# Block means of v from a second copy of v, added up on GpSimd

## The chip, the cores and the metric

The kernel runs on one core of a Trainium2 chip. The metric is the device time of one execution in microseconds (us), the median of several runs. Engines are named as the profile names them: PE is TensorE's matmul, PEld its weight load, DVE is VectorE, ACT is ScalarE, POOL is GpSimd, SP is SyncE, which issues most DMAs. An engine works through its own queue in order.

## The reference

Attention with a local window and block summaries, then a mixture of experts with greedy routing. Cut to what matters here:

```python
q, k, v: (4 batches, 8 heads, 768 positions, 64), float32
k_sum = k.reshape(B, H, 24, 32, 64).max(axis=3)     # 24 blocks of 32 positions
v_sum = v.reshape(B, H, 24, 32, 64).mean(axis=3)    # the block means
scores_l = scale * q @ k.T, only where |i - j| < 16
scores_s = scale * q @ k_sum.T + log(32)
a = softmax(concat([scores_l, scores_s]))
attn = a @ concat([v, v_sum])
# then: x = attn, 3072 rows of 512; logits = x @ w_gate (8 experts);
# greedy assignment, 384 rows for each expert; out = relu(x @ w1[e]) @ w2[e]
```

The change touches only how v_sum is worked out.

## The kernel before

Attention works on units u of 64 positions, 12 for a batch, 48 in all, in pairs that make a tile t of 128 positions, 24 in all. A unit sees 24 block keys and a window of 94 keys, so 118 columns. For every tile PE does the scores (task "s", line 316, 32 matmul records with 4 head pairs, 2 units, 2 halves and two passes), a transpose of the exponentials for each unit ("t", line 135), the value matmuls ("pv", line 352, tile names o0 and o1), a transpose of the output ("xt", line 135) and the routing logits ("l", line 358). DVE masks the scores and takes their maximum ("m", line 324), and normalises the output ("n", lines 378 to 381); ACT does the exponentials ("e", line 331). The copy of a transposed unit ("c", lines 175 and 177, which are in a helper) goes to ACT or DVE. A value matmul of tile t waits for "n" of tile t-1, since one pair of PSUM banks serves all tiles.

The windows of v lie in VW, one buffer for even and one for odd batches: rows 0 to 23 hold the 24 block means, rows 24 to 119 a unit's 96 positions of v, loaded by one DMA for each unit ("w", line 304, 195 KB). A 65th column of ones in each head gives the softmax sum.

The block means of a batch, for each half of the heads g: "vm" (lines 267 to 273), 12 matmuls over the loaded windows that add up the 32 positions of each block (in PSUM at four times 32 rows, 24 records in the profile since float32 takes two passes); "vmc", a copy to SBUF; "vb" (line 283), one matmul that puts the rows in block order; "vbc", a copy to rows 0 to 23 of unit 0. After the second half "place" (line 292) copies these rows on POOL to the other 11 units. So vm needs all 12 windows of its batch. Both halves take turns in the one PSUM bank "x", which the output transposes use too.

For each batch POOL also copies key windows ("win", 128x1128, line 177) and block maxima ("ks", 128x288, line 177) for batches 1 to 3, and issues the store of every output tile ("xw", line 418) to DRAM. The maxima themselves are DVE's ("max", line 252). Loads for the next batch run while a batch is worked on: q by one DMA of 1536 KB (batch 0 in three of 512 KB), k by four of 399 KB.

The order of the instructions on every engine is written by a planner (line 142): it keeps a list of tasks with an engine, a cost, dependencies and a rank, and takes, engine by engine, what can start earliest, and among those within a slack the lowest rank. The numbers in TUNE are ranks' offsets, slacks and the planner's lead LA. After attention come the routing rounds and the experts (lines 441 to 774); the change doesn't touch them.

Of the kernel before, what the change touches and what calls it, by code (L numbers as in the profile page):

```python
# [23 lines left out]
NB = S // BLK  # L24
# [13 lines left out]
    y2m=0.021, y3=1.7, y4=1.5, y5=1.6, y7=1.1, lo=1.1, sp=1.6, qx=23.421, aw=9.0, as_=2.6,  # L38
    ap=1.6, qf=8.3981, xw=5.4012, fp=2.4, ql=21.2102, mm=0.174, my=0.228, wlo=1.6, xlo=1.1, LA=4.6, PT=7, 
    sm=4, spe=0, sdve=0.327, sact=0.018, spool=0, m=0.309, e=1.649, t=1.965, c=0.695,  # L40
    n=0.518, xt=3.377, xf=3.627, l=5.806, k=18.158, q=15.15, vm=5, mx=9.243, back=3.94, w=12, qa=-11.877, qb=1.082, cut=22,
    cs=0.19, ct=0.45, cp=0.54, cx=0.45, cl=0.42, wend=22.685, wstart=1.0, wfrac=0.538,
# [6 lines left out]
CO = 128 + 3 * C  # L49
CA = CO + 96 + NB  # L50
CW = CA + E + 224
# [5 lines left out]
def attention_moe(ctx, tc, qT, kT, v65, wg, w1r, w2r, cst, out, dbg=None, dbi=None):  # L57
# [123 lines left out]
    with ExitStack() as att:  # L181
# [3 lines left out]
        VW = [sb.tile([128, NQ, H, VD], F32, name=f"vw{i}") for i in range(2)]  # L185
        kd, kw, VP, VM, VB, KS, SM, PS, PE_, PP, PT, PO, XS, XP, XTS, PL = ({} for _ in range(16))
        cuts = [0, 8, 16, TUNE['cut'], 24]
# [47 lines left out]
        for b in range(B):  # L235
# [7 lines left out]
            for p in range(HP):  # L243
# [19 lines left out]
                def _(eng=None, b=b, p=p):  # L263
                    copy(eng or nc.gpsimd, kw[b, p][:, :, :NB], KS[b, p][:, None, :].to_broadcast([128, NQ, NB]))

            for g in range(2):
                @task(("vm", b, g), "pe", 1.6, [("w", u0 + i) for i in range(NQ)] + ["constants"]
                      + ([("vbc", b, 0)] if g else [("xf", u0 // 2 - 4)] if b else []), u0 - TUNE["vm"] + 0.1 * g)
                def _(b=b, g=g):
                    VP[b, g] = psum.tile([128, 512], F32, name="x")[:, :4 * VD]  # L270
                    for k in range(3):
                        for j in range(4):
                            nc.tensor.matmul(VP[b, g][32 * j:32 * j + 32], own[:C, k], VW[b % 2][:C, 4 * k + j, 4 * g:4 * g + 4].rearrange("k h d -> k (h d)"), start=k == 0, stop=k == 2)  # L273

                @task(("vmc", b, g), {"act": 0.42, "dve": 0.4}, None, [("vm", b, g)], u0 - TUNE["vm"])
                def _(eng, b=b, g=g):
                    VM[b, g] = sb.tile([128, 4 * VD], F32, name="vm", bufs=2)
                    copy(eng, VM[b, g], VP[b, g])

                @task(("vb", b, g), "pe", 0.45, [("vmc", b, g)], u0 - TUNE["vm"])  # L280
                def _(b=b, g=g):
                    VB[b, g] = psum.tile([128, 512], F32, name="x")[:NB, :4 * VD]
                    nc.tensor.matmul(VB[b, g], blocks, VM[b, g], start=True, stop=True)
# [497 lines left out]
def _layouts(q, k, v, moe_w_gate, moe_w1, moe_w2):  # L781
# [69 lines left out]
```

## Time and profile before

| | |
|---|---|
| time, median of 3 runs | 503.75 us (500.2 to 506.34) |
| time of the profiled execution | 499.47 us |
| its span, first to last instruction | 497.7 us |
| busy: PE, PEld | 458.6 us (92%), 388.6 us (78%) |
| busy: DVE, ACT, POOL | 330.8 us (66%), 218.1 us (44%), 125.6 us (25%) |
| granted TensorE clock, mean | 0.957 |
| attention part | to about 139 us |

The page gives busy time by engine and a strip of 40 slices; the trace can be asked for busy time in a given stretch, for the chain of work that ended last, for an engine's instructions in order of time, and for groups of equal instructions with the mean time of one. A piece in a timeline may merge several instructions; "x24" is their number. Brackets at its end tell how long the engine was idle before it, and what ended that.

### The profile page before, as it was taken

How to read it: one execution, taken by the hardware profiler on the slowest of the kernel's cores; microseconds unless marked ns; L12 is line 12 of the kernel's file. 1: busy time of each engine (PE TensorE's matmuls, PEld its weight loads, DVE VectorE, ACT ScalarE, POOL GpSimd, SP SyncE). 2: the span in 40 equal slices, each digit the busy share in tenths (PEclk: the TensorE clock that was granted, in tenths of full speed). 3: DMA queues.
4: the chain of work that ended last, by engine and by line, in shares of the span. 5: the costliest groups of instructions: out<-in, count | busy, mean ns of one | idle time of the engine just before them, and what ended most of it. 6: DMA issues, size and time to landing. Idle time of an engine off the chain costs nothing.

```text
span 497.7 us, 13114 instructions
## 1 busy us (share of the span) xinstructions
PE 458.6 (92%) x5161; PEld 388.6 (78%) x5161; DVE 330.8 (66%) x1295; ACT 218.1 (44%) x454; POOL 125.6 (25%) x193
## 2 busy tenths in 40 slices
PE   5989999999945799989999999999998999999993
PEld 5568786878835798679779868978986998988982
DVE  4587989978767678749949867696795462461510
ACT  5575765877701433324324413333341553453410
POOL 9392745416122000121023005003100501302011
PEclk9998999999965799989999999999998999999998
DMA  8999978111203704615607408443434553621001
GB/s 273 320 325 375 297 244 265 67 66 45 87 24 136 267 1 171 233 63 183 221 28 257 184 1 296 128 161 119 146 110 146 165 175 138 197 88 63 2 21 42
DMA packets 24156, 76.27 MB, mean 153 GB/s; under 512 B 3488, under 2 KB 3744, under 8 KB 23712
## 3 DMA queue, kind: packets, MB, share of 16 engines
q1 hardware_dynamic: 18336, 56.58, 34.5%
q0 software_dynamic: 5760, 18.88, 10.8%
q8 instruction: 40, 0.66, 0.5%
q14 instruction: 20, 0.16, 0.1%
HBM read 62.86 MB, written 12.58 MB: 152 GB/s over the span
## 4 chain that ended last, share of the span: by engine, by line
PE 70%; DVE 11%; issue 8%; DMA 7%; SPq 2%; POOL 1%; POOLq 0%; ACT 0%; DVEq 0%; ACTq 0%
PE h L754 23%; PE y L771 18%; PE r L453 5%; PE o L352 5%; DMA vw<-v 5%; PE t L135 5%; PE s L316 4%; PE l L358 2%; PE x L135 2%; PE xt L135 2%; DMA xg<-xd,idx 2%; DVE al L598 2%; PE x L273 1%; DVE g L107 1%; SPq L304 1%
## 5 line engine op out<-in xcount | busy, mean ns | idle before, releaser
L771 PE MATMUL y<-bl,hh 128*128 128x512 f32 x192 | 79.0, 412 | 0.0
L737 POOL DMA_INDIRECT out<-y,idx x24 | 23.7, 986 | 215.7 <-ACT y L735 214.0
L771 PE MATMUL y<-bh,hl 128*128 128x512 f32 x192 | 77.5, 403 | 0.0
L771 PE MATMUL y<-bh,hh 128*128 128x512 f32 x192 | 77.1, 402 | 0.0
L758 ACT ACTIVATE hh<-h 128x384 fp32r<-128x384 f32 x64 | 31.5, 492 | 89.4 <-PE h L754 82.7
L331 ACT ACTIVATE pe<-sm,mx 128x118 f32<-128x118 f32 x192 | 57.6, 383 | 7.1 <-DVE mx L324 7.0
L754 PE MATMUL h<-xh,ah 128*128 128x384 f32 x256 | 58.4, 346 | 0.0
L754 PE MATMUL h<-xl,ah 128*128 128x384 f32 x256 | 58.3, 342 | 0.0
L754 PE MATMUL h<-xh,al 128*128 128x384 f32 x256 | 57.7, 344 | 0.0
L761 DVE SCALAR_TENSOR_TENSOR hl<-h,hh 128x384 fp32r<-128x384 f32 x64 | 35.3, 552 | 32.5 <-ACT hh L758 32.5
L629 ACT ACTIVATE xh<-xt 128x384 fp32r<-128x384 f32 x28 | 13.7, 491 | 80.8 <-PE xt L135 80.8
L754 PEld LDWEIGHTS h<-xh,ah 128*128 128x128 f32 x256 | 46.3, 192 | 0.7
L324 DVE CUSTOM_DVE_ANT_0 sm<-s,cs 128x118 f32<-128x118 f32 x192 | 40.6, 276 | 8.6 <-PE s L316 7.3
L754 PEld LDWEIGHTS h<-xh,al 128*128 128x128 f32 x256 | 45.6, 191 | 0.0
L754 PEld LDWEIGHTS h<-xl,ah 128*128 128x128 f32 x256 | 45.2, 189 | 0.0
L609 POOL DMA_INDIRECT xg<-xd,idx x24 | 24.1, 1003 | 79.9 <-DVE L L518 34.8
L595 ACT ACTIVATE ah<-raw 128x1024 fp32r<-128x1024 f32 (+1 forms) x36 | 32.4, 958 | 26.1 <-DVE m L124 21.5
L771 PEld LDWEIGHTS y<-bh,hh 128*128 128x128 f32 x192 | 36.7, 191 | 7.0
L771 PEld LDWEIGHTS y<-bl,hh 128*128 128x128 f32 x192 | 36.8, 192 | 6.0
L771 PEld LDWEIGHTS y<-bh,hl 128*128 128x128 f32 x192 | 36.7, 191 | 5.8
L453 PEld LDWEIGHTS <-g 128*128 128x128 bf16 x1008 | 29.0, 97 | 15.6 <-DVE g L107 7.9
L598 DVE TENSOR_TENSOR al<-raw,ah 128x1024 fp32r<-128x1024 f32 (+1 forms) x36 | 38.4, 1099 | 0.8 <-ACT ah L595 0.8
(130 smaller groups left out, 784.4 us busy)
## 6 DMA issues: line engine op xcount, KB each, us to landing
raw<-w1r SPq DMA_DIRECT2D x32, 512.0 KB, 4.4
raw<-w2r SPq DMA_DIRECT2D x32, 512.0 KB, 4.2
vw<-v SPq DMA_DIRECT2D x48, 195.0 KB, 7.9
kd<-kT SPq DMA_DIRECT2D x16, 399.0 KB, 5.8
xd<-x POOLq DMA_DIRECT2D x24, 256.0 KB, 4.2
qt<-qT SPq DMA_DIRECT2D x3, 1536.0 KB, 12.8
qt<-qT SPq DMA_DIRECT2D x3, 512.0 KB, 5.8
xg<-xd,idx POOLq DMA_INDIRECT x24, 3.7
```

What stands on the lines that cost most here:

```text
L135: nc.tensor.transpose(o, i, idn)
L324: nc.vector.tensor_tensor_reduce(sm[:, p], PS[u][:, p], m, -0.125, 3e38, op0=OP.add, op1=OP.min, accum_out=mx[:, p:p + 1])
L331: nc.scalar.activation(PE_[u][:, p], SM[u][0][:, p], AF.Exp, bias=SM[u][1][:, p:p + 1], scale=-1.0)
L352: nc.tensor.matmul(po(t, s)[x * 64:x * 64 + 64, p], PT[u][:, p, x * 64:x * 64 + 64], VW[b % 2][:C, i - s + x, 2 * p + s], start=True, stop ...
L453: nc.tensor.matmul(pc, g[t // HT][:, t % HT * n:t % HT * n + 128], oh[:, t], start=t == 0, stop=t == NT - 1)
L595: nc.scalar.activation(hi[:, c], raw[:, c], AF.Copy)
L598: nc.vector.tensor_tensor(lo[:, c], raw[:, c], hi[:, c].bitcast(F32), op=OP.subtract)
L609: nc.gpsimd.indirect_dma_start(out=x, out_offset=None, in_=xd, in_offset=bass.IndirectOffsetOnAxis(ap=idx[:, c:c + 1], axis=0))
L754: nc.tensor.matmul(ph, a[:, d], b[:, d], start=n == 0, stop=n == 11)
L758: nc.scalar.activation(hh[:, f], ph, AF.Relu)
L761: nc.vector.scalar_tensor_tensor(hl[:, f], ph, 0.0, hh[:, f].bitcast(F32), op0=OP.max, op1=OP.subtract)
L771: nc.tensor.matmul(py[c], a[:, f, s], b, start=f == 0 and i == 0, stop=f == 7 and i == 2)
```

## The change

For batches 1 to 3, "vm" and "vmc" go. A new DMA ("vt", 96 rows of 16,640 bytes, 1.6 MB) brings the batch's v once more, each of 96 rows holding 8 neighbouring positions. POOL adds these 8 up in four instructions ("va"): 4 positions of 8 onto others in two adds of 1040 elements, then 2 onto 2, then 1 onto 1 (520 elements). One matmul for each half of the heads ("vb") then adds groups of four rows with the new constant `quarters` (24 columns, 1/32 each). So the windows are no longer needed for the means. Batch 0 keeps its way, but the second half of the heads uses the PSUM bank "l" rather than "x", and the SBUF copy uses the buffer "xr". Several TUNE numbers differ, among them LA, the ranks of the window loads (w) and key maxima (mx), and two slacks; they move tasks within the planner's order.

```diff
-    ... LA=4.6, PT=7, 
-    sm=4, spe=0, sdve=0.327, sact=0.018, spool=0, m=0.309, e=1.649, t=1.965, c=0.695,
-    n=0.518, xt=3.377, xf=3.627, l=5.806, k=18.158, q=15.15, vm=5, mx=9.243, back=3.94, w=12, ...
+    ... LA=6.154, PT=7, 
+    sm=4, spe=0.015, sdve=0.316, sact=0.358, spool=0, m=0.569, e=2.793, t=2.307, c=0.793,
+    n=0.518, xt=3.377, xf=3.104, l=5.806, k=18.109, q=16.26, vm=5, vt=12, va=8, mx=12.906, back=6.52, w=5.302, ...
...
-CA = CO + 96 + NB
+CA = CO + 96 + 2 * NB
...
-    blocks = cs[:, CO + 96:CA]
+    blocks, quarters = cs[:, CO + 96:CO + 96 + NB], cs[:96, CO + 96 + NB:CA]
...
+            if b:
+                @task(("vt", b), "sp", 0.48, [("vb", b - 1, 1)] if b > 1 else [], u0 - TUNE["vt"], 4.35)
+                def _(b=b):
+                    VT[b] = sb.tile([96, 8, H * VD], F32, name="vt")
+                    v = v65[b]
+                    nc.sync.dma_start(VT[b], bass.AP(tensor=v.tensor, offset=v.offset + HALO * H * VD, ap=[[8 * H * VD, 96], [H * VD, 8], [1, H * VD]]))
+
+                for k, (i, j, n) in enumerate(((0, 4, 2), (2, 6, 2), (0, 2, 2), (0, 1, 1))):
+                    @task(("va", b, k), "pool", 2.4 if n == 2 else 1.25, [("va", b, k - 1) if k else ("vt", b)], u0 - TUNE["va"])
+                    def _(b=b, i=i, j=j, n=n):
+                        nc.gpsimd.tensor_tensor(VT[b][:, i:i + n], VT[b][:, i:i + n], VT[b][:, j:j + n], op=OP.add)
+
             for g in range(2):
-                @task(("vm", b, g), "pe", 1.6, [("w", u0 + i) for i in range(NQ)] + ["constants"]
-                      + ([("vbc", b, 0)] if g else [("xf", u0 // 2 - 4)] if b else []), u0 - TUNE["vm"] + 0.1 * g)
...
+                bank = "l" if b == 0 and g else "x"
+                for _ in range(b == 0):
+                    @task(("vm", b, g), "pe", 1.6, [("w", u0 + i) for i in range(NQ)] + ["constants"], u0 - TUNE["vm"] + 0.1 * g)
+                    def _(b=b, g=g, bank=bank):
+                        VP[b, g] = psum.tile([128, 512], F32, name=bank)[:, :4 * VD]
...
+                        VM[b, g] = sb.tile([128, 4, 128], F32, name="xr", bufs=2).rearrange("p a k -> p (a k)")[:, :4 * VD]
...
-                @task(("vb", b, g), "pe", 0.45, [("vmc", b, g)], u0 - TUNE["vm"])
...
+                @task(("vb", b, g), "pe", 0.5, [("va", b, 3), "constants", ("vbc", b, 0) if g else ("xf", u0 // 2 - 4)] if b else [("vmc", b, g)], u0 - TUNE["vm"] + 0.1 * g)
+                def _(b=b, g=g, bank=bank):
+                    VB[b, g] = psum.tile([128, 512], F32, name=bank)[:NB, :4 * VD]
+                    if b:
+                        nc.tensor.matmul(VB[b, g], quarters, VT[b][:, 0, 4 * g * VD:4 * (g + 1) * VD], start=True, stop=True)
+                    else:
+                        nc.tensor.matmul(VB[b, g], blocks, VM[b, g], start=True, stop=True)
...
+    for n in range(NB):
+        cst[4 * n:4 * n + 4, CO + 96 + NB + n] = 1.0 / BLK
```

How the order moves, at three places. First PE, around the block means of batch 1 (x is the PSUM bank, vw_101 the windows of odd batches, o the value matmuls, l the logits, t the transposes). Before:

```order
L358 MATMUL l<-wgs,xr 64x8 x8
L135 MATMUL t<-cs,pe 118x128 x8
L273 MATMUL x<-vw_101,cs 32x260 x12
L352 MATMUL o_986<-vw_100,pt 64x65 x8
L352 MATMUL o_987<-vw_100,pt 64x65 x8
L283 MATMUL x<-vm,cs 24x260
```

Now:

```order
L374 MATMUL l<-wgs,xr 64x8 x8
L135 MATMUL t<-cs,pe 118x128 x4
L368 MATMUL o_941<-vw_100,pt 64x65 x8
L297 MATMUL x<-vt,cs 24x260
L135 MATMUL t<-cs,pe 118x128 x4
```

Both stand at value tile 5: the group of 12 is gone, and the first of the two short matmuls of the batch comes between the halves of that tile, from vt.

Second POOL, from the key windows and maxima of batch 1 (kw<-kd, kw<-ks) to the placements of batch 1 (vw_101<-vw_101). Before:

```order
L418 DMA xd<-x 128x512 x2
L177 COPY kw<-kd 128x12x94 x2
L177 COPY kw<-ks 128x12x24
L418 DMA xd<-x 128x512
L177 COPY kw<-kd 128x12x94 x2
L177 COPY kw<-ks 128x12x24
L292 COPY vw_101<-vw_101 24x520 x11
```

Now:

```order
L434 DMA xd<-x 128x512 x2
L276 ISA
L276 TENSOR_TENSOR vt<-vt 96x1040 x3
L276 TENSOR_TENSOR vt<-vt 96x520
L434 DMA xd<-x 128x512 x2
L177 COPY kw<-kd 128x12x94 x2
L308 COPY vw_101<-vw_101 24x520 x11
```

The adds stand ahead of two stores and two window copies, and the placements behind these. "ISA" is a configuration instruction of POOL, which stood ahead of its first arithmetic after attention (line 441).

Third SP's queue, from the constants behind the first batch's windows on. Before:

```order
L247 DMA kd<-kT 128x798 x4
L241 DMA qt_98<-qT 128x1024
L241 DMA qt_99<-qT 128x3072
L304 DMA vw_101<-v 96x520 x12
L247 DMA kd<-kT 128x798 x4
```

Now:

```order
L247 DMA kd<-kT 128x798 x4
L241 DMA qt_99<-qT 128x3072
L241 DMA qt_98<-qT 128x1024
L271 DMA vt<-v 96x4160
L247 DMA kd<-kT 128x798 x2
L320 DMA vw_101<-v 96x520
L247 DMA kd<-kT 128x798
L320 DMA vw_101<-v 96x520
```

The second copy of v follows the q of batches 1 and 0; the windows of batch 1 come after it, one by one among the keys of batch 2. Two more pieces of the order are told in words: PE now has the scores of tile 3 between the two halves of value tile 0 (they stood ahead of both), and DVE has two key maxima of batch 1 and the masks of tile 3 ahead of the normalisation of tile 0.

## Rows read from the trace of the kernel before

**Rows 1.** The page, part 1: engine, busy us, share of the span, instructions.

```profile
PE 458.6 (92%) x5161; PEld 388.6 (78%) x5161; DVE 330.8 (66%) x1295; ACT 218.1 (44%) x454; POOL 125.6 (25%) x193
```

**Rows 2.** Busy us by stretch: length, five engines, PEclk, DMA share, GB/s.

```profile
20.00:30.00 10.00, 9.56 (x167) 6.22 (x170) 6.58 (x38) 5.77 (x18) 7.02 (x13) 1.00 1.03 403
30.00:40.00 10.00, 7.81 (x154) 6.65 (x143) 7.80 (x45) 6.97 (x21) 7.89 (x15) 0.94 1.05 288
40.00:50.00 10.00, 10.00 (x200) 8.35 (x202) 7.39 (x53) 6.88 (x20) 2.41 (x4) 0.89 1.02 378
...
59.00:85.50 26.50, 26.15 (x559) 20.83 (x560) 23.82 (x124) 18.34 (x54) 14.75 (x25) 1.00 0.87 271
85.50:114.50 29.00, 29.00 (x606) 23.21 (x608) 23.55 (x142) 21.70 (x63) 10.79 (x21) 1.00 0.16 59
```

**Rows 3.** The chain of waits in order of time: start us, us, what.

```profile
49.20 1.47 PE x L273 x24
...
51.74 0.55 PE x L283 x2
...
104.34 1.46 PE x L273 x24
```

**Rows 4.** PE's timeline: start us, us, instruction, idle before.

```profile
28.30 1.15 PE L352 MATMUL o<-vw,pt 118*64 118x65 f32 x32
29.39 1.04 PE L316 MATMUL s<-kw,qt 64*64 64x118 f32 x32
...
31.05 1.15 PE L352 MATMUL o<-vw,pt 118*64 118x65 f32 x32
...
34.12 0.91 PE L352 MATMUL o<-vw,pt 118*64 118x65 f32 x22
37.18 0.51 PE L352 MATMUL o<-vw,pt 118*64 118x65 f32 x10 [2.15 <-issue]
...
38.77 1.94 PE L135 MATMUL t<-cs,pe 128*118 128x128 f32 x8
40.65 1.87 PE L352 MATMUL o<-vw,pt 118*64 118x65 f32 x32
...
45.55 1.09 PE L135 MATMUL t<-cs,pe 128*118 128x128 f32 x8
```

**Rows 5.** Groups by form, 0 to 135 us: busy, mean ns | idle before.

```profile
L292 POOL COPY vw<-vw 24x520 f32<-24x520 f32 x44 | 25.0, 612 | 7.6 <-ACT vw L175 6.7 <-DVE vw L177 0.9
L252 DVE TENSOR_REDUCE ks<-kd 128x24 f32<-128x768 f32 x16 | 15.2, 948 | 5.8 <-DMA kd<-kT 5.8
L177 POOL COPY kw<-kd 128x1128 f32<-128x1128 f32 x12 | 13.2, 1134 | 1.2 <-DMA kd<-kT 1.2
L418 POOL DMA_DIRECT2D xd<-x x23 | 12.6, 550 | 41.7 <-DVE x L381 26.0 <-DVE mx L324 15.7
L177 POOL COPY kw<-ks 128x288 f32<-128x288 f32 x12 | 5.0, 433 | 6.8 <-DVE dn L378 3.1 <-DVE L L422 2.7 <-DVE ks L252 0.9
L177 DVE COPY vm<-x 128x260 f32<-128x260 f32 x5 | 2.1, 425 | 0.9 <-PE x L273 0.8
```

**Rows 6.** POOL's timeline: start us, us, instruction; the placements of batches 1 and 2.

```profile
57.53 6.24 POOL L292 COPY vw<-vw 24x520 f32<-24x520 f32 x11 [0.87 <-ACT vw L175]
...
83.67 6.24 POOL L292 COPY vw<-vw 24x520 f32<-24x520 f32 x11
```

**Rows 7.** Line 441 (duration min/median/max, first and last start), then POOL's timeline.

```profile
L441 POOLq MODIFY_POOL_CONFIG  x2: 37/37/37, 137.7 to 137.7; - x2
```

```profile
140.30 1.53 POOL L441 TENSOR_SCALAR count<-colsi 128x128 f16<-128x128 int16 x3 [2.64 <-PE l L358]
```

**Rows 8.** The page, part 6: DMA issues, KB each, us to landing.

```profile
kd<-kT SPq DMA_DIRECT2D x16, 399.0 KB, 5.8
...
qt<-qT SPq DMA_DIRECT2D x3, 1536.0 KB, 12.8
qt<-qT SPq DMA_DIRECT2D x3, 512.0 KB, 5.8
```

More of the change, by code (lines that the diff above doesn't have):

```diff
@@ L38 @@
     y2m=0.021, y3=1.7, y4=1.5, y5=1.6, y7=1.1, lo=1.1, sp=1.6, qx=23.421, aw=9.0, as_=2.6,
[L39 to L41 removed]
+    ap=1.6, qf=8.3981, xw=5.4012, fp=2.4, ql=21.2102, mm=0.174, my=0.228, wlo=1.6, xlo=1.1, LA=6.154, PT=7,
+    sm=4, spe=0.015, sdve=0.316, sact=0.358, spool=0, m=0.569, e=2.793, t=2.307, c=0.793,
+    n=0.518, xt=3.377, xf=3.104, l=5.806, k=18.109, q=16.26, vm=5, vt=12, va=8, mx=12.906, back=6.52, w=5.302, qa=-11.877, qb=1.082, cut=22,
     cs=0.19, ct=0.45, cp=0.54, cx=0.45, cl=0.42, wend=22.685, wstart=1.0, wfrac=0.538,
@@ L185, in attention_moe @@
         VW = [sb.tile([128, NQ, H, VD], F32, name=f"vw{i}") for i in range(2)]
-        kd, kw, VP, VM, VB, KS, SM, PS, PE_, PP, PT, PO, XS, XP, XTS, PL = ({} for _ in range(16))
+        kd, kw, VT, VP, VM, VB, KS, SM, PS, PE_, PP, PT, PO, XS, XP, XTS, PL = ({} for _ in range(17))
         cuts = [0, 8, 16, TUNE['cut'], 24]
@@ L264, in _ @@
                     copy(eng or nc.gpsimd, kw[b, p][:, :, :NB], KS[b, p][:, None, :].to_broadcast([128, NQ, NB]))
-            for g in range(2):
-                @task(("vm", b, g), "pe", 1.6, [("w", u0 + i) for i in range(NQ)] + ["constants"]
-                      + ([("vbc", b, 0)] if g else [("xf", u0 // 2 - 4)] if b else []), u0 - TUNE["vm"] + 0.1 * g)
[L269 to L278, printed above, removed]
-                @task(("vb", b, g), "pe", 0.45, [("vmc", b, g)], u0 - TUNE["vm"])
-                def _(b=b, g=g):
-                    VB[b, g] = psum.tile([128, 512], F32, name="x")[:NB, :4 * VD]
-                    nc.tensor.matmul(VB[b, g], blocks, VM[b, g], start=True, stop=True)
@@ new lines, in attention_moe, with _ @@
+            for g in range(2):
+                bank = "l" if b == 0 and g else "x"
[3 more added lines that the diff above has]
+                        VP[b, g] = psum.tile([128, 512], F32, name=bank)[:, :4 * VD]
+                        for k in range(3):
+                            for j in range(4):
+                                nc.tensor.matmul(VP[b, g][32 * j:32 * j + 32], own[:C, k], VW[b % 2][:C, 4 * k + j, 4 * g:4 * g + 4].rearrange("k h d -> k (h d)"), start=k == 0, stop=k == 2)
+                    @task(("vmc", b, g), {"act": 0.42, "dve": 0.4}, None, [("vm", b, g)], u0 - TUNE["vm"])
+                    def _(eng, b=b, g=g):
+                        VM[b, g] = sb.tile([128, 4, 128], F32, name="xr", bufs=2).rearrange("p a k -> p (a k)")[:, :4 * VD]
+                        copy(eng, VM[b, g], VP[b, g])
+                @task(("vb", b, g), "pe", 0.5, [("va", b, 3), "constants", ("vbc", b, 0) if g else ("xf", u0 // 2 - 4)] if b else [("vmc", b, g)], u0 - TUNE["vm"] + 0.1 * g)
[5 more added lines that the diff above has]
+                        nc.tensor.matmul(VB[b, g], blocks, VM[b, g], start=True, stop=True)
```

## The prediction

> **What bounds the kernel now.** Start with the page's busy shares: PE 92%, POOL 25% [rows 1]. A share over the whole span says little, so next come the stretches of the attention part [rows 2]. From 59.0 us on PE is busy 26.15 us of 26.50 and 29.00 of 29.00, while DVE has 23.82 and 23.55 and POOL 14.75 and 10.79: there PE's own work sets the pace. Before that the DMA engines are full (share 1.03 and 1.05 from 20 to 40 us), and PE has gaps. The chain of waits in order of time stays on PE and contains the block means of the later batches: pieces of 24 records, of which four lie on it, 1.45 to 1.47 us each; the first and the last but one are shown [rows 3]. The other two are batch 2's, in a stretch where PE is no less full. The short matmul behind each takes 0.55 us. Last, PE's timeline [rows 4]: at 35.03 us it stops for 2.15 us in the middle of the value matmuls of tile 2, put down to "issue". After that idle time eight transposes take 1.94 us where eight others take 1.09, and 32 value matmuls 1.87 where others take 1.15; the granted clock of the stretch 40 to 50 us is 0.89 [rows 2], part of it at the lower level, 1.2 GHz. That stop costs 2.15 + 0.85 + 0.72 = 3.7 us.
>
> **The change, part by part.** *Removed from PE:* six groups of 1.46 us = 8.8 us. All lie where PE has next to no idle time, so nothing else sets the pace there. The six copies between the two matmuls go too (0.43 us each on DVE [rows 5]); they lay in gaps of DVE and ScalarE, and I count nothing for them.
>
> *Kept on PE:* one 260-column matmul per half, now with 96 rows contracted in place of 128: 0.55 us as before.
>
> *Moved:* the first batch's second half. With a bank of its own it follows the first half directly. The first value matmul now has the scores of tile 3 (1.04 us [rows 4]) and eight transposes (1.09) less ahead of it, and PE's gap of 0.44 us between 20 and 30 us [rows 2] may close, so it can begin near 25.7 us rather than 28.30. Only the gap would be gain: the scores of tile 3 now come between the halves of value tile 0. The second value tile waits for DVE to normalise the first, and DVE now has two key maxima (0.95 us each [rows 5]) and eight score rows of tile 3 ahead of that. By the rows' durations this ends near 31.0 us, the very time at which value tile 1 begins now (31.05), when the kernel before has also put out the scores of tile 4 and four transposes, from 29.39 to 31.05 [rows 4]. So the new order is 1.7 us behind at that point.
>
> *Added on POOL:* per later batch three adds of 1040 elements and one of 520. The trace has no two-operand instruction of such a size. Copies of 520 and 1128 elements take 0.612 and 1.134 us [rows 5], that is 0.86 ns an element and 0.165 us fixed. If a second operand is free, a batch's adds take 3 x 1.06 + 0.61 = 3.8 us; if the operands are read one after the other, 3 x 2.12 + 1.22 = 7.6; twice that again, 15.2, is the upper bound. I take 7.6, since a second operand must be read. The Trainium skill (GPSIMD Engine Reference, Elementwise side-by-side cycle accounting) speaks against such adds on GpSimd: 2.6 cycles an element at 1.2 GHz; by that a batch's adds would take an estimated 8.5 us, and the sum would stay the same as long as this is hidden. No row here shows it.
>
> *What hides the adds.* For batch 1 they begin when the second copy of v is in. Ahead of it on SP's queue after 20 us stand 0.27 MB of constants, four key tiles, two 512 KB pieces of q and 1536 KB of the next q [rows 8], 4.3 MB, and two output tiles of x (0.5 MB) run beside; with its own 1.6 MB that is 6.6 MB. At 403 GB/s to 30 us and 288 after that [rows 2] it lands near 39 us. POOL itself comes free about then: from some 25 us, when the means of batch 0 are in, it has 11 placements, three window copies, three of the key maxima's and three stores of x, 6.7 + 3.4 + 1.3 + 1.7 = 13.1 us. So the adds end near 46.7 us. PE reaches their matmul after the first half of value tile 5: 31.0 us for tile 1, then four tiles at (29.00 - 2 x 1.46 - 2 x 0.55) / 6 = 4.16 us each [rows 2, 3], some 47.6 us. The adds are just in time, by 0.9 us.
>
> For batch 2 POOL's queue counts. From the placements of batch 1 (near 50.5 us) to those of batch 2 it holds 11 placements, six stores, five copies of maxima, four window copies and the adds: 6.7 + 3.3 + 2.2 + 4.5 + a = 16.7 + a. It was 26.1 us from the one to the other before (57.53 to 83.67 [rows 6]). PE wants batch 1's means for value tile 6 near 47.6 + 6.0 = 53.6 us (one and a half tiles on) and batch 2's 26.5 - 2.9 = 23.6 us later, at 77.2, and with a = 7.6 POOL is there at 74.8. A longer a counts twice by then (the adds of batch 1 and of batch 2), so POOL holds PE up from about a = 8.7 us on. Queued behind the adds are two stores of x and two window copies; four x tiles are in rotation, and the stores have a tile's time (4.16 us) to spare three times over. For batch 3 POOL's queue holds 14.1 + a (seven stores, three copies of maxima, two window copies) against PE's 29.0 - 2.9 = 26.1 us: slack.
>
> *Added transfers:* 3 x 1.6 MB. The second and third fall after 50 and 74 us; the DMA share from 85.5 to 114.5 us is 0.16 [rows 2]. The v windows now follow the copy one by one, as tiles need them. The constants grow by 24 columns, 12 KB: nothing.
>
> *The new bound.* Between 59.0 and 85.5 us DVE had 23.82 us of work. PE keeps 26.15 - 2.9 = 23.2, DVE 23.4 after one copy less: DVE is level with PE there, and as the two wait for each other by turns something is lost. Between 0 and 2.4 us (DVE at the 90% it had); I take 1.0.
>
> *The sum.* The stop of 2.15 us at "issue" belongs to no edit; whether it returns can't be read from one execution. At the first matmul of batch 1 the new order is 3.7 - 1.7 = 2.0 us ahead if it does not return, 1.7 behind if it does. So -8.8 - 2.0 + 1.0 = -9.8, or -8.8 + 1.7 + 1.0 = -6.1; I take the middle, -7.9, against the profiled execution's 499.47: 491.6. The four executions of the kernel before (500.2, 503.75, 506.34 and 499.47) have a mean of 502.4, 3.0 above the profiled one; for a median of runs I add this: **494.5**. Routing and experts after the attention part are unchanged and only begin earlier.
>
> **Rivals.**
> 1. *The first adds come late.* If the load runs at 288 GB/s from 20 us on, it lands near 42.9, the adds end at 50.5, PE waits 2.9 us, then runs at the lower clock for a while as after the stop at 35 us (1.6 us). For it: DMA is full there, and the two estimates lie within 1 us. Against: 403 GB/s is what the same stretch had, and PE may be late itself. 494.5 + 4.5 = 499.0.
> 2. *POOL becomes the bound: slower.* If a two-operand add costs four copies, a = 15.2, POOL misses batch 2 by 2 x (15.2 - 8.7) = 13.0 us and batch 3 by 14.1 + 15.2 - 26.1 = 3.2 more: 494.5 + 16.2 = 510.7. It is even with the kernel before near a = 12.4, and more than 1% slower from some 14.1. For it: POOL's queue has 1.8 us to spare ahead of batch 2. Against: copies run at 0.86 ns an element.
> 3. *POOL has to load code before the first add.* In the order a configuration instruction stands ahead of it. The trace has that instruction in 0.037 us at 137.7, and the first instruction behind it begins at 140.30, 2.6 us later, an idle time put down to PE's last logits [rows 7]; so a load costs under 2.6 us. If all of that counted, from 38.1 us on, the adds would begin at 40.7 and end at 48.3, 0.7 us late. Each us beyond costs one; with the adds 4.1 us late, and 1.6 us at the lower clock, it is 500.2, within 1%. The Trainium skill (GPSIMD Engine Reference, Instruction dispatch) states about 6 us for the first call of a freshly loaded kernel, by which they would be that late; the row at 140.30 does not bear this out.
> 4. *Several stops like that at 35 us.* Transfers last longer now (4.8 MB more); three stops at 3.7 us in place of the half I count give 494.5 + 9.3 = 504. For it: PE waited for nothing else there, while DMA was full. Against: one such stop in the whole attention part.
>
> **The numbers.** Forecast case 0.73 (its own range 490.5 to 498.5), rival 1 0.13, rival 2 0.05, rival 3 0.05, rival 4 0.04. About 1% (5 us) is what a measurement of this kernel can tell from no change. Faster by more than that: nearly all of the forecast case and a third of rival 1, 0.72. Slower: rival 2 and a piece of rival 4, 0.06. The rest, 0.22, is within 1%. The range of 8 in 10 takes the forecast case, rival 1 and the scatter of the runs: 489 to 500.5.
>
> **What would show it.** Right: from 59 us on PE stays over 98% busy, with 0.55 us matmuls alone for the block means; six tiles take near 23.5 us where they took 26.5; each add takes 2.1 to 2.4 us; the attention part ends 6 to 10 us earlier. Wrong: PE idle ahead of the new matmul by more than 1 us (rival 1 or 3; the adds' start tells which), placements behind a busy POOL with PE waiting (rival 2), more "issue" idle on PE (rival 4), or DVE without a gap while PE waits for normalised tiles or masked scores, which would mean that I put the price of the new order too low.

## The result and the profile after

The changed kernel takes **505.07 us** (median of 20 runs, 501.28 to 513.1), the kernel before 501.26 (20 runs, 499.48 to 507.78). The ratio is 1.0062, 95% interval 1.0034 to 1.0091: slower by 3 us, where 494.5 was forecast, and outside the range. (Ratios here leave disturbed runs out, so they are not always the quotient of two medians.) The profiled execution took 506.69 us, its span is 504.9, 7.2 longer than before. These two executions lie further apart than the typical ones: the one of before is 1.8 us under its median, this one 1.6 above. Nearly all of the 7.2 lies in the attention part, whose end (the first matmul of routing) moved from 139.75 to 146.82 us.

The page, part 1 (busy us, share, instructions), parts 2 and 3 (clock and DMA share in 40 slices of 12.6 us; DMA queues) and 6 (transfers) of the changed kernel:

```profile
PE 457.4 (91%) x5017; PEld 391.4 (78%) x5017; DVE 329.6 (65%) x1292; ACT 216.9 (43%) x451; POOL 150.3 (30%) x205
...
PEclk9997988979985679989999999999999999999997
DMA  8999999871110900841824715535425444621001
...
q8 instruction: 39, 0.64, 0.5%
...
vw<-v SPq DMA_DIRECT2D x48, 195.0 KB, 11.5
kd<-kT SPq DMA_DIRECT2D x16, 399.0 KB, 9.4
...
vt<-v SPq DMA_DIRECT2D x3, 1560.0 KB, 13.9
```

PE has 144 matmuls fewer than in [rows 1], yet hardly less busy time, and POOL has 25 us more. A key tile now takes 9.4 us to land, 5.8 in [rows 8]. The same stretches as in [rows 2] (length, busy us of five engines, PEclk, DMA share, GB/s):

```profile
20.00:30.00 10.00, 8.46 (x145) 5.91 (x144) 7.00 (x40) 7.07 (x22) 8.29 (x18) 1.00 1.07 408
30.00:40.00 10.00, 6.59 (x131) 5.50 (x131) 6.22 (x31) 4.44 (x13) 6.81 (x12) 0.93 0.97 242
40.00:50.00 10.00, 9.90 (x173) 8.68 (x177) 6.59 (x42) 4.96 (x16) 8.83 (x5) 0.73 1.04 342
...
59.00:85.50 26.50, 22.88 (x455) 19.65 (x454) 21.46 (x123) 19.50 (x57) 18.57 (x21) 0.89 1.02 278
85.50:114.50 29.00, 25.98 (x472) 21.68 (x471) 20.85 (x120) 18.96 (x54) 17.74 (x25) 0.87 0.78 222
```

Where PE was full before, it is idle for 3.62 and 3.02 us, and its clock is 0.89 and 0.87 where it was 1.00. No other engine is full: DVE, which I expected to be level with PE, has 21.46 of 26.50. But the DMA share is 1.02 and 0.78, where it was 0.87 and 0.16. PE's timeline (start us, us, instruction, idle before) shows four stops:

```profile
35.98 0.69 PE L332 MATMUL s<-kw,qt 64*64 64x118 f32 x3
40.10 1.84 PE L332 MATMUL s<-kw,qt 64*64 64x118 f32 x29 [3.44 <-issue]
...
66.28 0.64 PE L374 MATMUL l<-wgs,xr 128*64 128x8 f32 x16
68.44 1.32 PE L332 MATMUL s<-kw,qt 64*64 64x118 f32 x32 [1.52 <-issue]
...
80.22 0.67 PE L368 MATMUL o<-vw,pt 118*64 118x65 f32 x16
82.70 0.91 PE L135 MATMUL t<-cs,pe 128*118 128x128 f32 x4 [1.82 <-ACT pe L347]
...
97.11 0.66 PE L135 MATMUL x<-cs,x 128*128 128x128 f32 x4
100.78 1.46 PE L368 MATMUL o<-vw,pt 118*64 118x65 f32 x21 [3.02 <-POOL kw L177]
```

They add up to 9.80 us, against the one of 2.15 in [rows 4]. Two have no releaser. The other two name one, but the last is wrong on its face: a value matmul does not read the key windows (kw) that it names, and the placements that it does wait for had ended on POOL at 96.53 us.

**What the stops have in common.** Count TensorE's instructions (weight loads, matmuls, and the waits on semaphores between them) from the program's start. The four stops stand after 961, 1985, 2497 and 3009 of them, the one of before after 961: each is 193 plus a multiple of 256. And the queue that the page calls "instruction" moves packets of 16,384 bytes: 39 of them here, 40 before, for 10,169 and 10,415 instructions of TensorE, some 260 to a packet; with the 256 of the counts that is 64 bytes an instruction. So a stop stands where one block of instructions is used up and the next has not come. The trace's records of that queue, set against the time at which PE goes over from one block to the next:

| kernel | block that starts after | the one before it began | this block landed | PE goes on |
|---|---|---|---|---|
| before | 961 | 29.54 | 35.79 (6.25 later) | 37.18 |
| before | 1985 | 57.98 | 62.20 (4.22) | 63.82 |
| before | 3521 | 94.64 | 95.64 (1.01) | 100.30 |
| after | 961 | 30.26 | 38.94 (8.68) | 40.10 |
| after | 1985 | 60.26 | 67.01 (6.75) | 68.44 |
| after | 2497 | 75.48 | 81.34 (5.87) | 82.69 |
| after | 3009 | 91.34 | 99.48 (8.13) | 100.78 |
| after | 3521 | 108.52 | 109.61 (1.09) | 114.18 |

With idle DMA engines a block lands about 1 us after PE has begun the one ahead of it, nearly 5 us early. With full ones it takes 4 to 9 us, and PE goes on 1.2 to 1.4 us after it has landed. A block of 256 instructions is 5.3 to 7.4 us of work in before (from 961 on), so the stop comes once that time is exceeded. The kernel before was near it in several places without showing it: at 1985 its block was there 1.61 us ahead, 0.2 us more than where PE stands still.

The Trainium skill (Runtime: NRT & Kernel Launch, Instruction fetch mechanics) says that instructions come in 16 KiB blocks of 256, fetched while the current one runs, at a cost that is mostly hidden. The first half agrees with the 16,384 bytes and the count of 256. The second holds here where the DMA share is low (landing 1.09 us after the block before began) and fails where it is full (8.68, and PE stands still for 3.44 us).

**The account**, against before's span: the removed matmuls -8.8; stops 9.80 - 2.15 = +7.65; the start (busy time from 20 to 30 us, 9.56 against 8.46) +1.1. The clock: the time at its lower level, 1.2 GHz, is twice the missing share times the length, 1.4 + 5.4 + 5.8 + 7.5 = 20.1 us here, 1.2 + 2.2 = 3.4 in [rows 2]; before the fall, PE had stood still. The scores after the first stop take 1.84 us where [rows 4] have 1.04, so a us at that level loses 0.43, in all (20.1 - 3.4) x 0.43 = 7.2 at most. The sum is +7.15, measured +7.2. PE's own time bears out both halves: from 20 us to the first matmul of routing it is idle 12.8 us where it was 4.1 (+8.7, the stops and the start), and busy 114.0 where it was 115.6 (-1.65: the 8.8 removed, and 7.15 back through the clock). This accounts for the two profiled executions; the typical loss is 3 us, so by estimate the stops and the clock cost some 4 us less in a typical pair.

POOL's adds (groups by form, then its timeline), and DVE beside the second batch's:

```profile
L276 POOL TENSOR_TENSOR vt<-vt 96x1040 f32<-96x1040 f32 x9 | 21.5, 2406 | 1.9 <-DMA vt<-v 1.7
...
L276 POOL TENSOR_TENSOR vt<-vt 96x520 f32<-96x520 f32 x3 | 3.9, 1288 | 0.2
```

```profile
39.90 8.58 POOL L276 TENSOR_TENSOR vt<-vt 96x1040 f32<-96x1040 f32 x4 [1.66 <-DMA vt<-v]
...
73.22 0.54 POOL L434 DMA_DIRECT2D xd<-x  x1 [5.48 <-PE t L135]
73.78 8.62 POOL L276 TENSOR_TENSOR vt<-vt 96x1040 f32<-96x1040 f32 x4
82.35 0.56 POOL L434 DMA_DIRECT2D xd<-x  x1
82.91 1.14 POOL L177 COPY kw<-kd 128x1128 f32<-128x1128 f32 x1
```

```profile
80.97 0.17 DVE L124 TENSOR_SCALAR m<-best 128x8 int32<-128x8 int32 x1
81.05 0.22 DVE L116 TENSOR_TENSOR cand<-L,best 128x64 bf16<-128x64 f32 x1
81.18 2.89 DVE L125 SCALAR_TENSOR_TENSOR key<-best,m 128x8 int32<-128x8 int32 x1
84.00 0.18 DVE L117 TENSOR_TENSOR cand<-cand,WA 128x64 bf16<-128x64 bf16 x1
```

A batch's adds take 8.6 us. And an instruction of DVE on 8 columns, its neighbours 0.17 to 0.22 us long, takes 2.89: it ends at 84.07, and the window copy that follows POOL's adds at 84.05. The Trainium skill (SBUF — State Buffer, SBUF: two separate sides) says that DVE and GpSimd share a pair of ports that one of them holds for a whole instruction, and that a DVE instruction with two SBUF inputs then waits; the row agrees that it waits, but not that it waits for one instruction: it began beside the last add, which ended at 82.40, and ended with the copy behind it. The adds are not the only cause. In the kernel before, beside three window copies of POOL, a DVE instruction with one operand in SBUF took 1.98 us (DVE first, then POOL):

```profile
75.34 1.98 DVE L124 TENSOR_SCALAR m<-best 128x8 int32<-128x8 int32 x1
```

```profile
74.02 3.27 POOL L177 COPY kw<-kd 128x1128 f32<-128x1128 f32 x3
```

Over all profiles 15 instructions of DVE's routing pass on 8 or 64 columns took 0.9 us and more, and each ended 0.03 to 0.06 us after one of POOL's copies or adds. The masks, whose scores lie in PSUM, kept 0.27 to 0.28 us beside the adds.

### The profile page after: what moved, and what is told of

Same layout as the page of the kernel before. It is cut to its first block, busy times and chain, and to the rows that moved or that the text cites. A ratio compares the mean times of both kernels' runs of the same rounds, so it can differ in the third digit from the quotient of the medians.

```text
span 504.9 us, 12844 instructions
## 1 busy us (share of the span) xinstructions
PE 457.4 (91%) x5017; PEld 391.4 (78%) x5017; DVE 329.6 (65%) x1292; ACT 216.9 (43%) x451; POOL 150.3 (30%) x205
## 4 chain that ended last, share of the span: by engine, by line
PE 68%; DVE 9%; issue 9%; DMA 8%; POOL 3%; ACT 1%; POOLq 0%; SPq 0%; DVEq 0%; ACTq 0%
PE h L770 23%; PE y L787 19%; PE r L469 5%; PE o L368 5%; PE s L332 4%; PE t L135 4%; DMA qt<-qT 3%; DMA vw<-v 3%; PE x L135 2%; PE l L374 2%; DMA xg<-xd,idx 2%; PE xt L135 2%; DVE al L614 1%; POOL vw L308 1%; DVE g L107 1%
## 6 DMA issues: line engine op xcount, KB each, us to landing
vw<-v SPq DMA_DIRECT2D x48, 195.0 KB, 11.5
```

## Experiments

Three theories. **A:** the 4.8 MB keep the DMA engines full for longer, TensorE's blocks of instructions come late, and the lower clock follows. **B:** GpSimd's adds cost it, by POOL's time or through the shared ports. **C:** the new order (the numbers) costs it. Each ratio is against the kernel before, run beside it on the same chip (medians of before 502.35, 503.8, 503.21, 504.62, 511.2 and 510.12 us).

**Bytes and adds apart.** First the adds with an eighth of the bytes:

```diff
-                    VT[b] = sb.tile([96, 8, H * VD], F32, name="vt")
+                    VT[b] = VT0        # cleared once
-                    nc.sync.dma_start(VT[b], ... ap=[[8 * H * VD, 96], [H * VD, 8], [1, H * VD]]))
+                    nc.sync.dma_start(VT[b][:, :1], ... ap=[[8 * H * VD, 96], [H * VD, 1], [1, H * VD]]))
```

> The changed kernel with one of the eight positions of the second copy of v loaded (0.2 MB a batch in place of 1.6 MB; the other seven are zeros from a memory that was cleared at the start, so the block means of batches 1 to 3 are those of one position in eight and not right). GpSimd's adds, the matmuls and the order are as in the changed kernel. Theory A (the 4.8 MB keep the DMA queues full for longer, TensorE's 16 KB instruction fetches wait behind them, and the clock falls to 0.5 after each stop): the stops that end at 68.4 and 100.8 us go, the low clock after them too; 5.8 us of stops and about 6.8 us of low clock less, 492 to 497 us. Theory B (GpSimd's adds, through their time on POOL and the port shared with VectorE, cost what the matmuls give): as the changed kernel, 503 to 507 us. Theory C (the order by the new numbers is worse): the same, 503 to 507 us.

Measured: 495.32 us, ratio **0.9871** [0.982, 0.9923]. A, as it said. No stop stands at 35, 68 or 101 us; one of 1.52 at 49.99 and one of 1.03 at 74.08 are left. Then the bytes without the adds:

```diff
-                for k, (i, j, n) in enumerate(((0, 4, 2), (2, 6, 2), (0, 2, 2), (0, 1, 1))): ...
-                @task(("vb", b, g), "pe", 0.5, [("va", b, 3), ...
+                @task(("vb", b, g), "pe", 0.5, [("vt", b), ...
```

> The changed kernel without GpSimd's adds: the full 1.6 MB a batch is loaded, and the matmul takes one of the eight positions, so the block means of batches 1 to 3 are those of one position in eight and not right. Theory A: the three stops of TensorE of 1.5 to 3.4 us at 35 to 101 us stay, and the time is 502 to 506 us (the wait of 1.8 us at 82.7 us, which comes through VectorE from the adds, may go). Theory B: 26 us of POOL gone, 493 to 498 us. Theory C: 503 to 507 us.

Measured: 503.16 us, 1.0021 [0.9984, 1.0057]: the gain does not come back. The stops are there (3.73 us to 40.28, 1.04 to 67.86, 3.07 to 76.19, 1.30 to 100.13), after 961, 1985, 2241 and 3009 instructions. Both edits together (one position in eight loaded, no adds):

```diff
-                    nc.sync.dma_start(VT[b], ...
+                    nc.sync.dma_start(VT[b][:, :1], ...
-                for k, (i, j, n) in enumerate(((0, 4, 2), (2, 6, 2), (0, 2, 2), (0, 1, 1))): ...
```

> The changed kernel with one of eight positions loaded and no adds of GpSimd (the block means of batches 1 to 3 are those of one position in eight and not right): what is left of the change is 8.8 us of matmuls less. Theory A with a cost of the adds through the port that GpSimd and VectorE share (the kernel with adds has waits of 1.0 and 2.0 us behind VectorE at 74 and 80 us): 490.5 to 493.5 us. If the adds cost nothing where the queues have room: as the run with the small load and the adds, 494 to 496.5 us.

Measured: 492.57 us, **0.9783** [0.9718, 0.9848], 10.9 us under before: what the removed matmuls are worth with little in their way (one stop of 1.47 us is left, and before's own at 35 us is gone). So the bytes cost 1.9% with the adds (1.0062 against 0.9871) and 2.4% without; the adds cost 0.9% where the bytes are few (the two intervals overlap a little), and 0.4%, within the error, where they are many. B is at most a small second part. Its place is seen in the run with adds and few bytes, on PE (first) and DVE:

```profile
77.31 0.62 PE L299 MATMUL x<-vt,cs 96*24 96x260 f32 x2
79.89 1.40 PE L370 MATMUL o<-vw,pt 118*64 118x65 f32 x32 [1.96 <-DVE x L399]
```

```profile
75.17 2.90 DVE L117 TENSOR_TENSOR cand<-cand,WA 128x64 bf16<-128x64 bf16 x1
```

This wait stands after 2,623 instructions, so in the middle of a block: DVE's normalisation stands behind its routing pass, which was held up beside POOL.

**The bytes in the kernel before,** read by nobody:

```diff
+            if b:
+                @task(("vt", b), "sp", 0.48, [("vb", b - 1, 1)] if b > 1 else [], u0 - 12, 4.35)
+                def _(b=b): ... nc.sync.dma_start(VT[b], ...)
```

> The kernel before with the same load of 1.6 MB for each later batch, which nothing reads. Theory A: stops of TensorE of 1.5 to 3.5 us come at about 65 and 98 us, each with a granted clock of 0.5 for some 3 us behind it: 506 to 512 us. Theories B and C: nothing reads the data, and the matmuls, the adds and the numbers are those of before: 500 to 502.5 us.

Measured: 516.32 us, **1.0261** [1.0196, 1.0326]; A, and 4 us above its range. PE stops four times, after 961, 1729, 2497 and 2753 instructions; the second:

```profile
61.10 0.82 PE L323 MATMUL s<-kw,qt 64*64 64x118 f32 x21
64.86 0.66 PE L323 MATMUL s<-kw,qt 64*64 64x118 f32 x3 [2.94 <-issue]
```

The stop is in the middle of a tile's scores, with the same operands on both sides.

**The banks alone,** with the numbers and the means of before:

```diff
+                bank = "l" if b == 0 and g else "x"
-                    VP[b, g] = psum.tile([128, 512], F32, name="x")[:, :4 * VD]
+                    VP[b, g] = psum.tile([128, 512], F32, name=bank)[:, :4 * VD]
```

> The kernel before with the second half of the first batch's block means in another bank, and the table of constants that is longer by 24 columns; the numbers, the means of the later batches and the loads are those of before. Of the forecast's terms this is the start: 0 to 1.5 us less, 499.5 to 501.5 us. Theory C would have nothing to say here; if this alone were slower by over 1 us, the banks would be part of the loss.

Measured: 503.1 us, 1.0016 [0.9978, 1.0054]: no difference to be seen. Nothing of the loss, and no gain. The stop at 35 us is 4.00 us in its profile, with the loads of before, where before had 2.15: the loads alone do not set its size.

**The numbers alone,** and the numbers taken out of the change:

```diff
-    ... LA=4.6, ... mx=9.243, back=3.94, w=12, ...
+    ... LA=6.154, ... mx=12.906, back=6.52, w=5.302, ...
```

> The kernel before with the changed kernel's numbers for the order and nothing else. Theory C (the new order costs): 505 to 510 us. Theory A: the order by itself is no loss, 499 to 503 us.

Measured: 505.86 us, 1.0082 [1.0047, 1.0117]. A's figure missed and C's held: in the kernel before these numbers are a loss. The other way about, the whole change with the old numbers:

```diff
-    ... LA=6.154, ... vt=12, va=8, mx=12.906, back=6.52, w=5.302, ...
+    ... LA=4.6, ... vt=12, va=8, mx=9.243, back=3.94, w=12, ...
```

> The changed kernel's way for all later batches with the numbers of the kernel before for the order. Theory A (the bytes make the fetches late whatever the order): 502 to 510 us where before takes 502. Theory C (the new numbers are the loss in the changed kernel): without them 494 to 499 us.

Measured: 519.62 us, **1.017** [1.0114, 1.0227], 1.1% worse than the change with its own (and, with before at 510.12 here, just above A's range too). C falls for the changed kernel. The longest stop there is 5.09 us, after 961 instructions; another is DVE's, its line 117 taking 2.35 us at 84.78 beside the adds (79.81 to 88.43):

```profile
89.95 1.35 PE L369 MATMUL o<-vw,pt 118*64 118x65 f32 x20 [3.14 <-DVE x L398]
```

Why the new numbers cost the kernel before 0.8% was not found; its profiled run was the fastest of its twelve.

**Packets of 2,080 bytes** in place of 16,640:

```diff
-                    VT[b] = sb.tile([96, 8, H * VD], F32, name="vt")
+                    VT[b] = sb.tile([96, 8, H * VD + 2], F32, name="vt")[:, :, :H * VD]
...
-                    dn = sb.tile([128, 2, H], F32, name="dn", bufs=3)
+                    dn = sb.tile([128, 2, H], F32, name="dn", bufs=2)
```

> The changed kernel with the second copy of v in rows of 2,080 bytes that lie 8 bytes apart, so that the DMA moves it in packets of 2,080 bytes in place of 16,640. The bytes and all else are the same. Theory A (the bytes keep the queues full): as the changed kernel, 503 to 507 us. Theory D (a packet of 16,640 bytes holds up the fetch that is behind it, bytes alone would not): the stops at 68 and 101 us shrink to under 1 us, 496 to 500 us.

Not quite all else is the same: dn, a small buffer of the normalisation, has two copies in place of three, here and in every version below that has the new way for one or two batches, and in the one above with the old numbers. That was not run by itself; this run shows no loss with it.

Measured: 506.22 us, 1.006 [1.0018, 1.0101], as the changed kernel, with stops of 1.78 us to 70.90 and 2.48 to 102.10. D falls for the copy of v; q of the later batches still came in packets of 12,288 bytes, 384 of them, here as in both kernels.

**A full DMA where it was idle,** 14 loads of q and k that nothing reads, behind attention's last:

```diff
+            for j in range(14) if u == U - 1 else ():
+                @task(("extra", j), "sp", 0.48, [("s", 17), ("w", U - 1), ("win", 3, 3), ("max", 3, 3)] ...
```

> The kernel before with 5.7 MB of loads that nothing reads, put behind the last loads of attention into buffers that are free by then, so that the DMA is full from about 97 us for some 15 us, where before it was 0.03 to 0.24 busy; order and work of all engines' other instructions are as before. Theory A (TensorE's instruction fetches come late when the queues are full, whatever they carry): the fetches that land at 102 to 114 us in before land late, one to three stops of 1 to 3.5 us without a releaser stand there, with 3 to 7 us of clock 0.5: 505 to 512 us. Rival E (the stops come from data that arrive late, or from the order on SP's queue): no stop there, 500.5 to 504 us.

Measured: 503.17 us, 1.0022 [0.9985, 1.0059]. A's figure missed, and its statement with it: the DMA was full (the trace has 6.4 MB more than before, not 5.7) and PE did not stop there.

```profile
105.00:110.00 5.00, 5.00 (x114) 3.82 (x113) 4.05 (x25) 4.51 (x15) 0.76 (x2) 1.00 1.03 409
110.00:115.00 5.00, 5.00 (x110) 3.35 (x108) 3.04 (x20) 3.36 (x10) 0.32 (x1) 1.00 1.02 413
```

The blocks were late, though: the two that fell there landed 4.47 and 4.87 us after the one before had begun, where before had 1.60 and 0.09. But PE had 5.9 and 7.3 us of work in them, and went on 1.46 and 2.40 us after they had landed. A full share is not enough: **the block's landing plus some 1.3 us has to exceed the block's own work.** These loads ran at 409 GB/s; the stretches with stops in the changed kernel at 222 to 278, and there the blocks that PE stopped for took 5.9 to 8.7 us. What besides the share makes a block late is open.

**The new way where the DMA has room:** for batch 3 alone, with the numbers of before.

```diff
+            new = b in (3,)
-            if b:
+            if new:
```

> The kernel before with the new way of making block means for batch 3 alone (its 1.6 MB are loaded where the DMA share of before is 0.53 and less, from 80 us on), the numbers of before, and the second bank for the first batch. Theory A (bytes in a stretch where the queues are already full are what costs): PE loses 2.9 us of matmuls and no new stop comes: 498 to 500 us. Theory B2 (each batch's adds and load cost about what the matmuls give, wherever they are): 501 to 503 us.

Measured: 501.21 us, **0.9958** [0.992, 0.9995]: faster than both kernels, by 2.1 us of the 2.9 removed, though the interval ends just short of 1. No new stop came (before's at 35 us, 2.15, is the only one). The time itself, 501.21, is in B2's range and 1.2 above A's; before took 503.8 here. For batches 2 and 3, loads as early as in the change:

```diff
-            new = b in (3,)
+            new = b in (2, 3)
```

> The new way for batches 2 and 3 with the numbers of before, their loads 12 steps ahead of their batch (the run with 7 steps was 1.8% slower than before). Theory A with the port: the load of batch 2 falls at about 50 to 62 us in full queues and costs a stop of 1.5 to 2.5 us, but the adds of batch 2 end before VectorE's routing pass at 81 us: 499 to 504 us. If the 3.2 MB alone made the loss of the run with 7 steps: 508 to 512 us.

Measured: 505.86 us, 1.0026 [0.9981, 1.0071]; 1.9 us above A's range; six stops after 961 to 3265 instructions, 8.3 us in all, eat the 5.9 us. The same, loaded 5 steps later:

```diff
-    ... vt=12, va=8, ...
+    ... vt=7, va=5, ...
```

> The kernel before with the new way for batches 2 and 3, their loads put later (7 steps ahead of their batch in place of 12), the numbers of before, and the second bank for the first batch. Theory A: 5.9 us of matmuls less; the load of batch 3 falls in idle queues, that of batch 2 at about 65 to 75 us, where before's share is 0.71 to 0.96, so that one stop of up to 2 us with its low clock may come: 496 to 499 us. Theory B2: 501 to 504 us.

Measured: 510.52 us, 1.0179 [1.0108, 1.0251]. That is 11.5 us above A's range. Late loads mean late adds: they ran from 79.55 to 88.16 us, beside DVE's routing pass, where three instructions took 3.03, 2.35 and 1.42 us, and a block landed at 82.20, for a stop of 2.68. Three more stops at ends of blocks, the longest 4.26 us to 38.86, ahead of these loads, make 9.4 us with it. So a load put later left the full stretch only in part and met the ports as well; how much each cost was not parted. With batch 3 alone, but the new numbers:

```diff
-    ... LA=4.6, ... mx=9.243, back=3.94, w=12, ...
+    ... LA=6.154, ... mx=12.906, back=6.52, w=5.302, ...
```

> The new way for batch 3 alone, with the changed kernel's numbers for the order. Theory A: 2.9 us of matmuls less, and as in the run with the small load the queues have more room around 35 us, so that the stop there is shorter: 496 to 500 us. Theory C: 503 to 507 us.

Measured: 508.52 us, 1.01 [1.0037, 1.0164]; A's figure missed, and it is 1.5 us above C's. With batch 3 alone the new numbers cost 1.4% (1.01 against 0.9958); they help only where the whole change is made. Its stops are after 961, 1473 and 2497 instructions (1.22, 2.62, 3.17 us).

**Small transfers.** The change with the second copy in eight pieces, and q in three:

```diff
+                    for j in range(8):
+                        nc.sync.dma_start(VT[b][:, j:j + 1], bass.AP(... offset=v.offset + (HALO + j) * H * VD, ...))
-            return [(n, n + FIRST) for n in range(0, NQ, FIRST)] if b == 0 else [(0, NQ)]
+            return [(n, n + FIRST) for n in range(0, NQ, FIRST)]
```

> The changed kernel with the second copy of v loaded in eight pieces of 195 KB in place of one of 1,560 KB, and q of the later batches in three parts of 512 KB. The bytes are the same. If a fetch waits behind the one large transfer that is ahead of it: the fetches land 1 to 3 us earlier, the stops of the changed kernel shrink to under 1 us, 497 to 501 us. If it waits behind whatever is queued (1.1 to 1.7 MB moved between the end of a block and the start of the next fetch in the traces so far, with large transfers and small): 503 to 507 us.

Measured: 502.23 us, **0.9954** [0.9908, 1.0001]; against 1.0062 for the same bytes in large transfers, with intervals that don't meet. The stretches of the version in pieces, as above:

```profile
59.00:85.50 26.50, 23.95 (x474) 19.11 (x476) 23.22 (x128) 18.38 (x53) 18.16 (x20) 1.00 1.04 302
85.50:114.50 29.00, 27.17 (x590) 23.28 (x590) 23.92 (x153) 23.01 (x68) 20.99 (x26) 1.00 0.76 227
```

The DMA share is as high, but the blocks land 4.1 to 6.5 us after the one before has begun, not 3.9 to 8.7; the longest stop is 2.32 us, and the clock stays at 1.00. There are five stops of 0.86 us and more at ends of blocks, 7.34 us in all against 9.80, so between these two profiles more was won by the clock than by the stops. (This profiled execution is 4.3 us under its median, the changed kernel's 1.6 above.) So of the 1.9% that the bytes cost in the changed kernel, some 1.1% goes with the form of the transfers. That a shorter queue ahead of the fetch does it fits, but the order of q's loads and its packets (4,096 bytes in place of 12,288) changed with it, and these were not parted. Batch 3 alone, with k and q loaded later:

```diff
-    ... k=18.158, q=15.15, ...
+    ... k=14, q=11, ...
```

> The new way for batch 3 alone, with k loaded 14 and q 11 steps ahead of their batch (before 18.2 and 15.2), so that the small loads of v of a batch come ahead of its q. If the stop at 35 us hangs on q's 1.5 MB that are queued just ahead: it shrinks by 1 us and more, 497 to 500 us. If the queue is full there whatever the order: as the run for batch 3 alone, 0.2 to 0.6% under before, 500 to 502.5 us.

Measured: 500.98 us, **0.9949** [0.9911, 0.9987], as good as with the old leads, and again faster than both kernels; the stop at 35 us shrinks to 0.81, but two others of 1.16 and 1.89 come, and the time is that of the second case. The last three, taken later, when all versions took some 8 us more: this version in pieces, the same for two batches, and small transfers of q with these leads in the kernel before. First batch 3:

```diff
+                    for j in range(8):
+                        nc.sync.dma_start(VT[b][:, j:j + 1], ...
-            return [(n, n + FIRST) for n in range(0, NQ, FIRST)] if b == 0 else [(0, NQ)]
+            return [(n, n + FIRST) for n in range(0, NQ, FIRST)]
```

> The new way for batch 3 alone with k loaded 14 and q 11 steps ahead, and all large transfers in pieces: the second copy of v in eight of 195 KB, q in three of 512 KB. If small transfers shorten the wait of the instruction fetches here as they did in the changed kernel: 497 to 500.5 us. If that came of something else: as with large transfers, 500 to 503 us.

Measured: 511.27 us, 1.001 [0.9975, 1.0046]. Two batches:

```diff
-            new = b in (3,)
+            new = b in (2, 3)
```

> The same pieces and leads with the new way for batches 2 and 3. The 1.6 MB more fall in queues that are full until some 70 us, and 2.9 us of matmuls go: 497 to 503 us if the fetches keep up, 504 us and more if they bound the blocks there.

Measured: 508.62 us, 0.9955 [0.9919, 0.9991], where large transfers, with the old leads, gave 1.0026 and 1.0179 (the first interval overlaps this one a little). The kernel before:

```diff
-    ... k=18.158, q=15.15, ...
+    ... k=14, q=11, ...
-            return [(n, n + FIRST) for n in range(0, NQ, FIRST)] if b == 0 else [(0, NQ)]
+            return [(n, n + FIRST) for n in range(0, NQ, FIRST)]
```

> The kernel before with q of the later batches in three parts of 512 KB and the leads of 14 and 11 steps, and nothing of the change. If the gain of the last two versions is the smaller and later transfers alone: 499 to 501 us. If it is the new way for batch 3: as before, 502.5 to 505 us.

Measured: 513.28 us, 1.0001 [0.9954, 1.0049]. Pieces of q by themselves give nothing; pieces help where the extra bytes of two or three batches are. That batch 3 alone gained 0.5% with large transfers and nothing with small ones is within reach of the two intervals, and open.

Over all twenty profiles, 52 stops of 0.75 us and more from 20 to 130 us have no releaser, and every one stands after 193 plus a multiple of 256 instructions and ends 1.1 to 1.7 us after a block has landed. Seven more stand at such a count and name an engine. The other 14 of that size stand at other counts, and each names an engine or a DMA.

## Why the prediction was wrong

- **The added transfers: the step that failed.** I put the second and third copy at nothing, because they "fall after 50 and 74 us" and the share from 85.5 to 114.5 us was 0.16. It became 0.78: the third copy came in from 90.8 to 99.0 us, the windows of v moved later with the copies, and the queue was full to 107 us (share 1.05 from 100 to 107). The bytes, in these large transfers, cost 1.9 to 2.4%, 10 to 12 us, where the sum had nothing; that is more than the 8.8 that the matmuls give.
- **The stop at "issue".** I took half of it into the sum as if it were chance, and gave several such stops 0.04 (rival 4, 504 us: the case that happened, by its mechanism; that its time is off by only 1 us is in part luck: it counts 2.5 stops more at 3.7 us, the profile shows three more at up to 5.0). The ground against it, "one such stop in the whole attention part", was the wrong count: what counts is how close the other blocks came, and four more of before's were there only 1.6 to 2.3 us ahead of PE. Nor was it chance whether it came: 18 of the 20 profiles have a stop of 0.75 us and more after 961 instructions, and only the two versions with an eighth of the bytes do not.
- **The removed matmuls, -8.8:** borne out, though not measured alone. PE has the 144 records less, and few bytes and no adds give -10.9, in which before's own stop is gone too. The new matmuls run with no idle time before them and take as long as the short ones of before.
- **The start:** value tile 1 waits 1.50 us for its normalisation, as worked out, and begins at 29.99 where I had 31.0. That is 1 us earlier than forecast. The 2.0 us of the sum's better end stood for a stop that does not return; it returned, with 3.44 us.
- **The adds:** 8.6 us a batch, not 7.6; the estimate from the cycles of the Trainium skill (GPSIMD Engine Reference, Elementwise side-by-side cycle accounting), 8.5, was the better one. They were hidden: the first end at 48.48 us, the matmul behind them runs at 52.41 without a wait (rival 1 did not come). That was luck in part: they end 1.8 us later than forecast, and PE came to that matmul 4.8 us later, behind its stop. Two things were left out. The second batch's adds stand behind a store of x that waited 5.48 us; and DVE's routing pass beside them, to which the version with few bytes loses some of its 0.9%.
- **The first copy** landed at 39.82 us, forecast near 39. Right (the 4.3 MB in its working should be 4.5; the total of 6.6 that it goes on with has that).
- **DVE level with PE, +1.0:** it did not get there, since PE was slower.
- **Rivals 2 and 3** fell. POOL is not the bound. The configuration instruction runs at 38.23 us and the first add begins at 39.90, 0.08 us after its data: a code load of over 1.6 us would show, and none does.
- **The lower clock** was in rival 4's 3.7 us a stop; measured, (7.65 + 7.2) / 3 = 5.0 at most for each stop more.

## What to carry to other kernels

Ahead of adding bytes to a stretch, look where its DMA share stands near 1 and whether an engine with thousands of instructions has idle time there that nothing releases; count its instructions up to such stops, and if the counts agree modulo a block, further bytes there can cost that engine time even when nothing waits for them (4.8 MB that nothing read cost 2.6%). Try DMA in stretches that have room (for the one batch whose copy falls there the change paid 0.4 to 0.5% in two versions, and nothing in pieces), and, where more bytes have to go through a full stretch, small transfers. And look what DVE does beside GpSimd's long instructions: short ones that read SBUF were held up here, the masks on scores in PSUM were not.

## What the runs showed of the hardware

- TensorE's instructions come in blocks of 16,384 bytes (256), about one block ahead: in the changed kernel a block lands 1.1 to 1.7 us after the block before has begun where the DMA share is under 0.4, 3.9 to 8.7 where it is near 1, and where PE has to stop for it, it goes on 1.1 to 1.7 us after the landing.
- A wait's named releaser can be wrong there: 7 of the 59 stops at a block's end name an engine ("POOL kw", "ACT pe", "DVE key").
- The size of the second copy's packets doesn't matter for this (1.006 with 2,080 bytes); a DMA share of 1.03 at 409 GB/s made no stop, one of 0.97 at 242 GB/s one of 3.44 us.
- An 8-column instruction of DVE with one operand in SBUF takes up to 3.03 us beside GpSimd's adds, 1.98 beside its copies in the kernel before, and 0.17 elsewhere.
